# Probabilities and MLP rows transposed in 32x32 blocks by VectorE in a two-layer decode kernel

## The chip, the cores and the metric

The kernel runs on one core of one Trainium2 chip. The metric is the device time of one execution in microseconds (us). Three runs of the kernel before gave a median of 722.28 us (722.20 to 722.33). A difference of 0.2% (1.4 us) is about what such runs can tell from no change.

## The reference

Four tokens (batch B = 4, one position each) of width D = 640 go through attention, MLP, attention, MLP, each behind a layer norm and added to the residual. Both attentions use the same cache and weights, and both MLPs the same weights. All data are fp32.

```python
# Hq = Hkv = 32, Dh = 128, Sk = 4096, W = 1024 (the last 1024 positions of the cache)
def _A_ref(x, k_cache, v_cache, wq, wo):
    q = (x @ wq).reshape(B, 1, 32, 128).transpose(0, 2, 1, 3)
    k, v = k_cache[:, :, Sk - W:, :], v_cache[:, :, Sk - W:, :]
    p = softmax(einsum("bhqd,bhkd->bhqk", q, k) * Dh ** -0.5)
    return einsum("bhqk,bhkd->bhqd", p, v).transpose(0, 2, 1, 3).reshape(B, 1, 4096) @ wo
def _B_ref(x, w1, w2):                      # w1: 640 x 1728, w2: 1728 x 640
    return einsum("bsf,fd->bsd", maximum(einsum("bsd,df->bsf", x, w1), 0), w2)

x = x + _A_ref(layernorm(x), ...); x = x + _B_ref(layernorm(x), ...)
x = x + _A_ref(layernorm(x), ...); x = x + _B_ref(layernorm(x), ...)
```

The keys of each head differ per batch entry, so one head needs four products of one row with 128 x 1024 keys, and four of one row of 1024 probabilities with 1024 x 128 values.

## The kernel before, in words

**Data.** The host packs each head into a record of 128 partitions by 9472 columns (REC): the head's part of wq (columns 0 to 640), the keys (640 to 4736, in two halves), the values (4736 to 8832, in two halves) and the head's part of wo (8832 to 9472). That is 4736 KB. The program reads 32 records for layer 0, then w1 and w2, then 27 records for layer 1 and w1 and w2 again.

**Buffers.** Five slots hold a record each; a `ring` of RING columns holds the weights of the first MLP and some pieces of layer 1. The last five heads of layer 0 stay in their slots, and layer 1 begins with these (the resident heads). The sixth head of layer 1 comes into the ring, in the pieces of IN_RING, while the first MLP still runs; the seventh to the eleventh come in pieces into whatever part of slots and ring has become free. From the twelfth head on whole records go into slots again; the first of them, into slot 2, needs room that the sixth and the seventh head use to their end.

**Order.** Every engine's instructions are chained in the order in which the code is written (class `InOrder`, whose line L81 stands on nearly every row of the profile). All loads are issued by SP, one after another in the fixed list `items`. `pump()` issues the next as soon as its columns are free in the program's order: `done(...)` behind each group of matmuls frees them. A load whose room isn't free holds up all behind it.

**One head.** `query` multiplies the normalized x (columns `xT`) with wq: the result has the four batch rows, split over four column groups of the PE array. VectorE scales it (`qs`), `query_T` transposes it on PE, and a VectorE sum over the groups gives the columns `qT`. `scores` does eight 128x512 matmuls into `sc_ps`, VectorE takes the maximum, ScalarE the exponentials with their sum (`exponentials`, into `prob`). `weights_T` transposes the probabilities with eight PE transposes, `values` multiplies them with the value blocks (`o_ps`), VectorE divides by the sum (`on`), `output_T` transposes with four PE transposes, and `project` adds to `acc`, which stays in PSUM and collects the layer's residual. The loop in `decode_kernel` is software-pipelined: `scores` of the next head is ahead of `values` of this one, and `query` is two heads ahead.

**MLP.** `center` subtracts the mean, `mlp` does x @ w1 into PSUM, relu by ScalarE into SBUF, PE transposes of the hidden rows, and 54 weight tiles of w2 (TILES). `busy` issues matmuls whose result is not used, between the real ones.

Of the kernel before, what the change touches and what calls it, by code (L numbers as in the profile page):

```python
# [47 lines left out]
NS = 5  # L49

TILES = [(f, n) for t in range(4) for f in range(t, 13, 4) for n in range(NB)]
# [3 lines left out]
RING = 4 * FF + 5 * FD  # L55

W1_RING = [0, FF, 2 * FF, 3 * FF, 0]
W2_RING = [(5, 4 * FF), (10, FF), (11, FF + 10 * FD), (11, FF + 21 * FD), (10, 0), (3, FF), (4, FF + 3 * FD)]
# [30 lines left out]
def decode_kernel(ctx: ExitStack, tc: tile.TileContext, xf, rec, w1, w2, out):  # L89
# [5 lines left out]
    ident = sb.tile([P, P], F32, name="ident")  # L95
    mean_of = sb.tile([P, P], F32, name="mean_of")
    xT = sb.tile([P, FD], F32, name="xT")
    prob = sb.tile([P, W], F32, name="prob")
    hidden = prob[:, :512]
    xc = prob[:, 512:512 + FD]  # L100
    square = prob[:, 768:768 + FD]
    pT = sb.tile([P, 2, B, 4], F32, name="pT")
    on = sb.tile([P, 4 * DH], F32, name="on")
    x_sb = on[:, :FD]
    ones = on[:, 2 * P:3 * P]
    hT = on[:, FD:FD + 4 * NB * B].rearrange("p (t j b) -> p t j b", t=4, j=NB)
    oTs = sb.tile([P, LATE, B], F32, name="oTs")
    qs = sb.tile([P, DH], F32, name="qs")
    qT = sb.tile([P, B, 4], F32, name="qT")
    small = sb.tile([P, 24], F32, name="small")  # L110
    nmax, rtot, rstd, eps, unused, sums, squares, tot0, tot1 = (small[:, i:i + 1] for i in range(9))
    var, std, raw = (small[:, i:i + B] for i in (12, 16, 20))
# [4 lines left out]
    sc_ps = ps.tile([P, W], F32, name="sc_ps")  # L117
    pt_ps = [ps.tile([P, 4, P], F32, name=f"pt_ps{i}") for i in range(2)]
    o_ps = ps.tile([P, 512], F32, name="o_ps")
    q_ps = ps.tile([P, 512], F32, name="q_ps")  # L120
# [4 lines left out]
    for n in range(NB):  # L125
        act.dma_start(x_sb[32 * n:32 * n + B], xf[B * n:B * n + B])
    pool.memset(ident, 1.0)
    pool.affine_select(ident, ident, pattern=[[1, P]], compare_op=OP.is_equal, fill=0.0, base=0, channel_multiplier=-1)

    folded = ident.rearrange("p (j s) -> p s j", j=NB).unsqueeze(1).to_broadcast([P, NB, 32, NB])  # L130
    dve.tensor_reduce(mean_of.rearrange("p (j s) -> p j s", j=NB), folded, op=OP.add, axis=AX.X)
    dve.tensor_scalar(mean_of, mean_of, 1.0 / D, None, op0=OP.mult)
    dve.memset(small, EPS)
    dve.memset(q_ps[:, :DH], 0.0)
    dve.memset(sc_ps, 0.0)
    dve.memset(o_ps, 0.0)

# [105 lines left out]
    def busy(n):  # L243

        pe.matmul(sc_ps[0:1, :n], ident[:, 0:1], slot[home(LAST, 0)][:, K:K + n], start=True, stop=True)

    def center(fill):

        x = acc[:, :FD]
        dve.memset(ones, 1.0)  # L250
# [9 lines left out]
        act.activation(square, xc, AF.Square, accum_out=squares)  # L260
        dve.tensor_copy(x_sb, x)

    def scale(before_exp):
# [3 lines left out]
        if before_exp:  # L267
            act.activation(unused, eps, AF.Exp)

    def scale_columns():  # L270

        dve.tensor_scalar(var, mean_of[:, :B], squares, None, op0=OP.mult)
        pe.matmul(o_ps[:, :B], ones, var, start=True, stop=True)
        act.activation(std, o_ps[:, :B], AF.Sqrt, bias=eps, scale=1.0)
# [4 lines left out]
    def residual():  # L279
        pe.matmul(acc[:, :FD], ident, x_sb, start=True, stop=False, skip_group_check=True)  # L280

    def query(r, h, first=False):
        key = ("rec", r, h)
        for k in range(KB):
            j = 32 * (k % NB)
            pe.matmul(q_ps[j:j + B, :DH], xblock(k), cols(key, WQ + k * DH, DH),
                      start=(k < NB), stop=(0 < k % NB or k == NB), skip_group_check=True)
        done(key, WQ, K)
        if first:
            scale_columns()  # L290
            dve.tensor_copy(qs, q_ps[:, :DH])
            dve.reciprocal(std, std)
        else:
            dve.tensor_scalar(qs, q_ps[:, :DH], rstd, DH ** -0.5, op0=OP.mult, op1=OP.mult)

    def query_T(first=False):
        pe.transpose(misc[:, :P], qs, ident)
        q = misc[:, :P].rearrange("p (j s) -> p s j", j=NB)[:, :B, :]
        if first:
            scale(True)  # L300
            dve.tensor_reduce(raw, q, op=OP.add, axis=AX.X)
            raw4, std4 = (a.unsqueeze(2).to_broadcast([P, B, 4]) for a in (raw, std))
            dve.scalar_tensor_tensor(qT, raw4, DH ** -0.5, std4, op0=OP.mult, op1=OP.mult)
            dve.reciprocal(rstd, rstd)
        else:
            dve.tensor_reduce(qT, q.unsqueeze(2).to_broadcast([P, B, 4, NB]), op=OP.add, axis=AX.X)

    def scores(r, h):
# [6 lines left out]
        dve.tensor_reduce(nmax, sc_ps, op=OP.max, axis=AX.X, negate=True)  # L315

    def exponentials(s):
        act.activation(prob, sc_ps, AF.Exp, bias=nmax, scale=1.0, accum_out=tot[s])

    def weights_T(i):  # L320
        for c in range(4):
            pe.transpose(pt_ps[i][:, c, :], prob[:, 512 * i + 128 * c:512 * i + 128 * c + 128], ident)
        dve.tensor_copy(pT[:, i], pt_ps[i].rearrange("p c (b s) -> p b c s", b=B)[:, :, :, 0])

    def values(r, h, s):
        key = ("rec", r, h)
        for i in range(2):
            for b in range(B):
                pe.matmul(o_ps[32 * b:32 * b + 4, :], pT[:, i, b, :], cols(key, V + VH * i + 512 * b, 512),
                          start=(i == 0), stop=(i == 1))  # L330
            done(key, V + VH * i, V + VH * i + VH)
        dve.reciprocal(rtot, tot[s])
        dve.tensor_scalar(on, o_ps, rtot, None, op0=OP.mult)

    def output_T(i):

        for c in range(4):
            pe.transpose(misc[:, P * c:P * c + P], on[:, DH * c:DH * c + DH], ident)
        m = misc[:, :]
        picked = bass.AP(tensor=m.tensor, offset=m.offset, ap=[m.ap[0], [32, B], [P + 1, 4]])  # L340
        dve.tensor_reduce(oTs[:, i], picked, op=OP.add, axis=AX.X)
# [8 lines left out]
    def mlp(r):  # L350
        h_ps = pt_ps[0].rearrange("p c n -> p (c n)")
        for k in range(KB):
            for j in range(NB):
                n = min(512, FF - 512 * j)
                pe.matmul(h_ps[32 * j:32 * j + B, :n], xblock(k), cols(("w1", r), k * FF + 512 * j, n),
                          start=(k == 0), stop=(k == KB - 1))
            done(("w1", r), k * FF, k * FF + FF)
            if k == 0:
                scale(False)
                dve.reciprocal(rstd, rstd)  # L360
                residual()
# [113 lines left out]
```

## Time and profile before

| | |
|---|---|
| median of three runs | 722.28 us (722.20 to 722.33) |
| profiled execution | 722.16 us, its span 720.2 us |
| PE (matmul) busy | 533.4 us, 74% of the span |
| VectorE busy | 208.9 us, 29% |
| ScalarE busy | 90.8 us, 13% |
| DMA queue of SP | 98.9% of 16 engines' span, 303.91 MB |
| HBM read | 303.84 MB, 422 GB/s over the span |
| mean granted PE clock | 0.853 |

The profiled execution's own time is 1.96 us longer than its span, which goes from the first to the last instruction. The names in the rows are those of the kernel's tiles without numbers: `slot<-rec` is a load of a record or a part of one, `ring<-w` one of MLP weights into the ring, `sc_ps` the scores, `pt_ps` the transposed probabilities or the hidden rows, `o_ps` the values' product, `misc` the transposes of `qs` and `on`, `acc` projection or w2. PE is TensorE's matmuls, PEld its weight loads, DVE VectorE, ACT ScalarE.

### The profile page before, as it was taken

Reading aid. Unit: us, or ns where it says so; the run is one execution under the profiler, and the core shown is the slowest. Engines: PE = TensorE matmul, PEld = TensorE weight load, DVE = VectorE, ACT = ScalarE, POOL = GpSimd, SP = SyncE. Lnnn points to the kernel's source line nnn. Section 1 sums busy time; section 2 is a strip of 40 time slices with the busy share of each in tenths; the row PEclk is TensorE's granted clock in tenths of the full one; section 3 lists DMA queues with packets and bytes.
Section 4 is the critical chain, followed back from the end, with each engine's and each line's share of the span. In section 5 each row is a group of like instructions: output and inputs, shape, how many; then the busy total and the mean of one; then the engine's idle time right before and its main releaser. Section 6 shows DMA issues by size and latency. Waiting matters only on the chain.

```text
span 720.2 us, 9962 instructions
## 1 busy us (share of the span) xinstructions
PE 533.4 (74%) x4428; PEld 220.2 (31%) x4428; DVE 208.9 (29%) x554; ACT 90.8 (13%) x156; POOL 0.7 (0%) x6
## 2 busy tenths in 40 slices
PE   3466767668676777767989889785767768677888
PEld 1132323223223232323324333232322323233332
DVE  3222232232332323233422343422223232232430
ACT  2101010110110101011111121201011010110110
POOL 0000000000000000000000000000000000000000
PEclk9778787887886878788999999987788888787999
DMA  9999999999999999999999999999999999999996
GB/s 375 433 437 437 435 433 422 426 432 436 436 433 422 426 436 437 432 430 417 420 401 395 416 429 428 438 432 432 426 431 434 432 432 430 426 432 422 428 420 274
DMA packets 15194, 304.54 MB, mean 423 GB/s; under 512 B 1697, under 2 KB 1969, under 8 KB 5297
## 3 DMA queue, kind: packets, MB, share of 16 engines
q1 hardware_dynamic: 15120, 303.91, 98.9%
q8 instruction: 34, 0.56, 0.3%
q14 instruction: 8, 0.06, 0.0%
q10 hardware_dynamic: 32, 0.01, 0.0%
HBM read 303.84 MB, written 0.08 MB: 422 GB/s over the span
## 4 chain that ended last, share of the span: by engine, by line
DMA 77%; PE 19%; DVE 2%; issue 1%; ACT 0%; SPq 0%; DVEq 0%; ACTq 0%
DMA slot<-rec 76%; PE sc_ps L81 4%; PE acc L81 4%; PE o_ps L81 3%; PE misc L81 3%; PE pt_ps L81 3%; PE q_ps L81 2%; DVE on L81 1%; DMA ring<-w 1%; DVE oTs L81 1%; DVE small L81 0%; ACT prob L81 0%; SPq L81 0%; SPq L78 0%; ACT small L81 0%
## 5 line engine op out<-in xcount | busy, mean ns | idle before, releaser
L81 PE MATMUL q_ps<-slot,xT 128*4 128x128 f32 x620 | 46.9, 317 | 142.4 <-DMA slot<-rec 141.5
L81 ACT ACTIVATE prob<-sc_ps,small 128x1024 f32<-128x1024 f32 x64 | 71.3, 1115 | 563.6 <-DVE small L81 547.8
L81 PE MATMUL sc_ps<-slot,qT 128*4 128x512 f32 x992 | 134.0, 663 | 1.3 <-ACT prob L81 0.7
L81 PE MATMUL o_ps<-slot,pT 128*4 128x512 f32 x1014 | 120.6, 592 | 2.3 <-DMA slot<-rec 1.3
L81 DVE TENSOR_REDUCE small<-sc_ps 128x1 f32<-128x1024 f32 x64 | 78.4, 1224 | 129.7 <-PE sc_ps L81 129.7
L81 PE MATMUL pt_ps<-ident,prob 128*128 128x128 f32 x518 | 112.6, 362 | 0.0
L81 PEld LDWEIGHTS pt_ps<-ident,prob 128*128 128x128 f32 x518 | 83.3, 188 | 29.3 <-issue 28.3
L81 PEld LDWEIGHTS q_ps<-slot,xT 128*4 128x4 f32 x620 | 20.7, 88 | 197.9 <-DMA slot<-rec 185.5
L81 DVE TENSOR_SCALAR qs<-q_ps,small 128x128 f32<-128x128 f32 x62 | 21.6, 348 | 141.4 <-PE q_ps L81 141.4
L81 PE MATMUL misc<-ident,on 128*128 128x128 f32 x256 | 54.6, 350 | 9.5 <-DVE on L81 9.5
L81 DVE COPY pT<-pt_ps 128x16 f32<-128x16 f32 x128 | 22.1, 174 | 122.5 <-PE pt_ps L81 122.5
L81 DVE TENSOR_SCALAR on<-o_ps,small 128x512 f32<-128x512 f32 x64 | 48.0, 750 | 30.2 <-PE o_ps L81 30.2
L81 PEld LDWEIGHTS o_ps<-slot,pT 128*4 128x4 f32 x1014 | 25.3, 87 | 83.7 <-issue 76.5
L81 PE MATMUL acc<-slot,oTs 128*4 128x160 f32 x512 | 38.3, 383 | 16.2 <-DVE oTs L81 16.2
L81 PEld LDWEIGHTS misc<-ident,on 128*128 128x128 f32 x256 | 34.7, 172 | 31.5 <-DVE on L81 16.9
L81 PEld LDWEIGHTS sc_ps<-slot,qT 128*4 128x4 f32 x992 | 20.8, 89 | 70.1 <-issue 64.7
L81 PE MATMUL misc<-ident,qs 128*128 128x128 f32 x64 | 23.6, 368 | 1.1 <-DVE qs L81 1.1
L81 PE MATMUL sc_ps<-slot,ident 128*1 128x512 f32 (+1 forms) x54 | 22.5, 513 | 0.0
L81 DVE TENSOR_REDUCE oTs<-misc 128x4 f32<-128x16 f32 x64 | 11.2, 174 | 33.3 <-PE misc L81 33.3
L81 PEld LDWEIGHTS acc<-slot,oTs 128*4 128x4 f32 x512 | 7.1, 84 | 36.5 <-DVE oTs L81 35.7
L81 DVE TENSOR_REDUCE qT<-misc 128x16 f32<-128x64 f32 x62 | 13.9, 224 | 2.4 <-PE misc L81 1.0
L81 PEld LDWEIGHTS misc<-ident,qs 128*128 128x128 f32 x64 | 12.6, 198 | 2.1 <-DVE qs L81 2.0
(59 smaller groups left out, 108.9 us busy)
## 6 DMA issues: line engine op xcount, KB each, us to landing
slot<-rec SPq DMA_DIRECT2D x46, 4736.0 KB, 31.2
slot<-rec SPq DMA_DIRECT2D x17, 2368.0 KB, 20.7
slot<-rec SPq DMA_DIRECT2D x5, 1024.0 KB, 32.7
ring<-w SPq DMA_DIRECT2D x5, 864.0 KB, 13.5
slot<-rec SPq DMA_DIRECT2D x2, 2048.0 KB, 42.5
slot<-rec SPq DMA_DIRECT2D x3, 1344.0 KB, 7.6
slot<-w SPq DMA_DIRECT2D x3, 864.0 KB, 31.3
ring<-rec SPq DMA_DIRECT2D x1, 2368.0 KB
```

The costliest lines, as they stand in the source:

```text
L81: r = build(*args, **kwargs)
```

## The change

- **Scores.** The query is computed as columns: wq is the stationary operand and x the moving one, so `misc` gets the 128 x 4 result and one VectorE copy makes `qT`. `scores` broadcasts one query column to 32 stationary columns, so that each batch entry fills 32 equal rows. The layer norm's scale and Dh ** -0.5 move into the exponential (`scale=rstd`), with one VectorE product for the bias. There are two buffers `sc_ps`, and the exponentials stay in PSUM.
- **Probabilities.** `weights` replaces `weights_T`: two VectorE transposes of 128x512 in 32x32 blocks from PSUM to PSUM (`t_ps`), each followed by a product with `mrt`, which holds 1 / sum and a mask of the batch entry. A value block then holds 32 keys of each of the four batch entries, and `values` has 16 stationary columns.
- **Output.** `values` leaves four diagonal blocks in `o_ps`; four VectorE instructions pick and add them (`on`), and one matmul with the matrix `pick` replaces four transposes.
- **MLP.** x @ w1 in four equal quarters of 432 columns; relu in PSUM; two VectorE transposes (224 and 256 columns) instead of four PE transposes and two copies; w2 packed to match.
- **Residual.** `acc` simply stays in PSUM; the copy `x_sb` and the matmul `residual` of each layer go.
- **Ring.** 8960 columns instead of 7712, in the room of `prob`, `ident` and others. The five w1 blocks have places of their own, w2 pieces and IN_RING are laid out anew, with six ring pieces (8320 columns) of the sixth head where there were five (7296).

PE in two heads of layer 1 before. `pt_ps` are the probability transposes, `misc<-ident,on` those of the output, `misc<-ident,qs` that of the query:

```order
L81 MATMUL o_ps<-slot_73,pT 4x512 x8
L81 MATMUL q_ps<-slot_75,xT 4x128 x5
L81 MATMUL misc<-ident,on 128x128 x4
L81 MATMUL acc<-slot_73,oTs 4x160 x4
L81 MATMUL pt_ps_78<-ident,prob 128x128 x4
L81 MATMUL misc<-ident,qs 128x128
L81 MATMUL pt_ps_79<-ident,prob 128x128 x4
L81 MATMUL sc_ps<-slot_75,qT 4x512 x8
L81 MATMUL o_ps<-slot_74,pT 4x512 x8
L81 MATMUL q_ps<-slot_71,xT 4x128 x5
```

And the same place now:

```order
L85 MATMUL sc_ps_77<-slot_74,qT 32x512 x8
L85 MATMUL o_ps<-slot_73,scratch 16x512 x8
L85 MATMUL misc<-xT,slot_75 128x4 x5
L85 MATMUL o_ps<-pick,scratch 128x4
L85 MATMUL acc<-slot_73,oTs 4x160 x4
L85 MATMUL sc_ps_78<-slot_75,qT 32x512 x8
L85 MATMUL o_ps<-slot_74,scratch 16x512 x8
```

The thirteen transposes of a head are gone, one `pick` matmul is new, and a head's projection is followed at once by the `scores` of the next but one.

VectorE in one head of layer 1 before, from the maximum of the scores (`small<-sc_ps`) on:

```order
L81 TENSOR_REDUCE small<-sc_ps 128x1
L81 RECIPROCAL small<-small 128x1
L81 TENSOR_SCALAR on<-o_ps,small 128x512
L81 TENSOR_SCALAR qs<-q_ps,small 128x128
L81 TENSOR_REDUCE oTs<-misc 128x4
L81 COPY pT<-pt_ps_78 128x16
L81 TENSOR_REDUCE qT<-misc 128x16
L81 COPY pT<-pt_ps_79 128x16
```

And now, where `scratch` is `on` in the block pick (128x128) and the stationary weights `wT` in the products (128x64):

```order
L85 TENSOR_REDUCE small<-sc_ps_78 128x1
L85 TENSOR_TENSOR small<-small 128x1
L85 TENSOR_SCALAR scratch<-o_ps,of_block 128x128
L85 SCALAR_TENSOR_TENSOR scratch<-o_ps,of_block,scratch 128x128 x3
L85 RECIPROCAL small<-small 128x1
L85 TENSOR_SCALAR mrt<-of_batch,small 128x4
L85 STREAM_TRANSPOSE t_ps<-sc_ps_78 128x512
L85 TENSOR_TENSOR scratch<-t_ps,mrt 128x64
L85 STREAM_TRANSPOSE t_ps<-sc_ps_78 128x512
L85 TENSOR_TENSOR scratch<-t_ps,mrt 128x64
L85 COPY qT<-misc 128x4
L85 COPY oTs<-o_ps 128x4
```

Eight instructions became fourteen, and `oTs` (this head's output, which `project` reads) now stands last, behind the next head's transposes.

The diff, cut to its core:

```diff
-TILES = [(f, n) for t in range(4) for f in range(t, 13, 4) for n in range(NB)]
+TILES = [(m, n) for m in range(13) for n in range(NB)]
-RING = 4 * FF + 5 * FD
+RING = 5 * FF + 2 * FD
-W1_RING = [0, FF, 2 * FF, 3 * FF, 0]
+W1_RING = [0, FF, 2 * FF, 3 * FF, 4 * FF]
-IN_RING = [(0, 1664, FF + 10 * FD), (1664, 3200, FF + 21 * FD), (3200, 4224, FF + 21 * FD + 1536),
-           (4224, 5760, 0), (5760, 7296, 1536)]
+IN_RING = [(0, 1152, 7680), (1152, 3200, 640), (3200, 4736, 2688), (4736, 6272, 4224), (6272, 7808, 5760),
+           (7808, 8320, 0)]
...
+    def query(r, h):
+        key = ("rec", r, h)
         for k in range(KB):
+            pe.matmul(misc[:, 8:8 + B], cols(key, WQ + k * DH, DH), xblock(k), start=(k == 0), stop=(k == KB - 1))
         done(key, WQ, K)
+        dve.tensor_copy(qT, misc[:, 8:8 + B])
...
-                pe.matmul(sc_ps[32 * b:32 * b + 4, 512 * i:512 * i + 512], qT[:, b, :],
+                pe.matmul(sc_ps[s][32 * b:32 * b + 32, 512 * i:512 * i + 512], qT[:, b:b + 1].to_broadcast([P, 32]),
...
+        dve.tensor_tensor(nmax, nmax, rstd, op=OP.mult)
+        act.activation(sc_ps[s], sc_ps[s], AF.Exp, bias=nmax, scale=rstd, accum_out=tot[s])
+
+    def weights(s):
+        dve.reciprocal(rtot, tot[s])
+        dve.tensor_scalar(mrt, of_batch, rtot, None, op0=OP.mult)
+        for i in range(2):
+            dve.transpose(t_ps, sc_ps[s][:, 512 * i:512 * i + 512])
+            dve.tensor_tensor(wT[:, i], t_ps.rearrange("p (c j) -> p c j", j=32)[:, :, :B],
+                              mrt.unsqueeze(1).to_broadcast([P, 16, B]), op=OP.mult)
...
-        dve.reciprocal(rtot, tot[s])
-        dve.tensor_scalar(on, o_ps, rtot, None, op0=OP.mult)
+        dve.tensor_scalar(on, o_ps[:, :DH], of_block[:, 0:1], None, op0=OP.mult)
+        for c in range(1, 4):
+            dve.scalar_tensor_tensor(on, o_ps[:, DH * c:DH * c + DH], of_block[:, c:c + 1], on, op0=OP.mult, op1=OP.add)
     def output_T(i):
+        pe.matmul(o_ps[:, :B], on, pick, start=True, stop=True)
+        dve.tensor_copy(oTs[:, i], o_ps[:, :B])
...
         for n, h in enumerate(hs):
             more = n + 1 < H
             i = n - (H - late)
             if more:
+                scores(r, hs[n + 1], (n + 1) % 2)
+            values(r, h)
+            if more:
+                weights((n + 1) % 2)
             if n + 2 < H:
                 query(r, hs[n + 2])
             if i < 0:
                 output_T(0)
                 project(r, h, 0, False)
```

More of the change, by code (lines that the diff above doesn't have):

```diff
@@ L243, in busy @@
     def busy(n):
-        pe.matmul(sc_ps[0:1, :n], ident[:, 0:1], slot[home(LAST, 0)][:, K:K + n], start=True, stop=True)
+        pe.matmul(sc_ps[1][0:1, :n], mean_of[:, 0:1], slot[home(LAST, 0)][:, K:K + n], start=True, stop=True)
     def center(fill):
         x = acc[:, :FD]
-        dve.memset(ones, 1.0)
         dve.tensor_reduce(sums, x, op=OP.add, axis=AX.X)
@@ L276, in xblock, with scale_scores @@
+    def scale_scores():
+        pe.matmul(o_ps[:, 8:8 + B], ones.to_broadcast([P, P]), mrt, start=True, stop=True)
+        dve.tensor_tensor(mrt, o_ps[:, 8:8 + B], of_batch, op=OP.mult)
+        dve.tensor_reduce(sums, mrt, op=OP.add, axis=AX.X)
+        act.activation(rstd, sums, AF.Sqrt, bias=eps_dh, scale=float(DH))
+        act.activation(unused, eps, AF.Exp)
     def xblock(k):
         return xT[:, 32 * k:32 * k + B]
[L279 to L280 removed]
@@ L320, in weights_T @@
[L320 to L325, printed above, removed]
+        dve.tensor_reduce(nmax, sc_ps[s], op=OP.max, axis=AX.X, negate=True)
+        if first:
+            dve.reciprocal(rstd, rstd)
+        dve.tensor_tensor(nmax, nmax, rstd, op=OP.mult)
+        act.activation(sc_ps[s], sc_ps[s], AF.Exp, bias=nmax, scale=rstd, accum_out=tot[s])
@@ L396, in decode_kernel @@
     pump()
-    residual()
+    pe.matmul(acc[:, :FD], ident, x_sb, start=True, stop=False, skip_group_check=True)
     for r in range(2):
@@ L401, in decode_kernel @@
         center(r > 0)
-        query(r, hs[0], True)
-        query_T(True)
-        scores(r, hs[0])
-        exponentials(0)
-        residual()
+        dve.tensor_scalar(mrt, mean_of[:, :B], squares, None, op0=OP.mult)
+        query(r, hs[0])
+        scale_scores()
+        scores(r, hs[0], 0, True)
         query(r, hs[1])
+        weights(0)
         for n, h in enumerate(hs):
```

152 lines of the change are left out of this document (52 added, 100 removed).

## The prediction

> **What bounds the kernel now.** I read the page's slices first, then the chain of waits, then the DMA queue's own issues.
>
> ```profile
> DMA  9999999999999999999999999999999999999996
> GB/s 375 433 437 437 435 433 422 426 432 436 436 433 422 426 436 437 432 430 417 420 401 395 416 429 428 438 432 432 426 431 434 432 432 430 426 432 422 428 420 274
> ...
> slot<-rec SPq DMA_DIRECT2D x46, 4736.0 KB, 31.2
> ```
>
> The DMA engines never rest before the last slice. A record (4736 KB, 4.85 MB) takes 11.3 us at the usual 430 GB/s. It lands 31.2 us after its issue, so it waits some 20 us behind others in the queue. Through most of the program compute could be many microseconds slower and no transfer would start later. The only low slices are numbers 21 and 22 (401 and 395 GB/s), from 360 to 396 us: the MLP of layer 0 and the start of layer 1. There the chain of waits leaves the DMA for compute:
>
> ```profile
> 406.00 1.83 PE sc_ps L81 x16
> ...
> 411.33 0.46 PE acc L81 x8
> ...
> 412.92 1.83 PE sc_ps L81 x16
> ...
> 446.02 0.46 PE acc L81 x8
> ...
> 453.47 26.66 DMA slot<-rec
> ```
>
> These are the resident heads. Layer 1 begins with five heads whose records still lie in the slots, so compute runs ahead at its own pace: 6.92 us a head (412.92 less 406.00), against 11.3 us that the DMA needs for one. The DMA now waits for room, and room comes from finished heads. How much slack is there? The columns are start, length (for several issues, first to last), what.
>
> ```profile
> 425.72 0.33 SPq L81 DMA_DIRECT2D slot<-rec  x1
> ...
> 437.28 0.33 SPq L81 DMA_DIRECT2D ring<-rec  x1
> 437.66 9.21 SPq L81 DMA_DIRECT2D slot<-rec  x2
> ```
>
> The DMA view gives, for the issue at 425.72 and for the program's very first one, KB and us to landing:
>
> ```profile
> slot<-rec SPq DMA_DIRECT2D x1, 2368.0 KB, 20.7
> ...
> slot<-rec SPq DMA_DIRECT2D x1, 2368.0 KB, 8.3
> ```
>
> So the piece issued at 425.72 landed at 446.4. Two more such pieces (437.28 and 437.66) end the queue at 446.4 + 11.3 = 457.7. The next load, the first whole record of layer 1 into slot 2, was issued at 446.5 (second of the two at 437.66), right after the seventh head's output projection (446.02 + 0.46). So it had 457.7 - 446.5 = 11.2 us to spare. The very first DMA takes 8.3 us where 2368 KB in the stream take 5.65, so a restart from an empty queue costs 2.6 us. True slack: 8.6 us. The forecast turns on whether the new heads use it up.
>
> **The larger ring: a gain.** The dips, per 2 us (last number GB/s, the one before DMA share):
>
> ```profile
> 370.00:372.00 2.00, 2.00 (x14) 0.70 (x14) 0.16 (x1) 0.26 (x1) 0.00 (x0) 1.00 0.92 315
> ...
> 382.00:384.00 2.00, 2.00 (x26) 0.72 (x19) 0.00 (x0) 0.00 (x0) 0.00 (x0) 1.00 1.01 411
> 384.00:386.00 2.00, 2.00 (x36) 0.82 (x35) 0.00 (x0) 0.00 (x0) 0.00 (x0) 1.00 1.00 319
> ...
> 388.00:390.00 2.00, 1.96 (x15) 0.75 (x14) 0.55 (x2) 0.00 (x0) 0.00 (x0) 1.00 0.93 357
> ...
> 396.00:398.00 2.00, 1.04 (x9) 0.36 (x13) 0.42 (x2) 1.21 (x2) 0.00 (x0) 1.00 1.00 382
> ```
>
> Against 411 GB/s the four lose 0.47 + 0.45 + 0.26 + 0.14 = 1.3 us. With 8960 columns the fifth w1 block no longer waits for the first, and the first two ring pieces of layer 1 need w2 pieces consumed earlier. I take all 1.3 us as gained (ends 0 and 1.3): the queue's end moves from 457.7 to 456.4.
>
> **The head: a loss.** Rows that price it (mean ns follows the busy time):
>
> ```profile
> L81 DVE TENSOR_REDUCE small<-sc_ps 128x1 f32<-128x1024 f32 x64 | 78.4, 1224 | 129.7 <-PE sc_ps L81 129.7
> L81 DVE TENSOR_SCALAR on<-o_ps,small 128x512 f32<-128x512 f32 x64 | 48.0, 750 | 30.2 <-PE o_ps L81 30.2
> L81 DVE COPY pT<-pt_ps 128x16 f32<-128x16 f32 x128 | 22.1, 174 | 122.5 <-PE pt_ps L81 122.5
> L81 DVE TENSOR_SCALAR qs<-q_ps,small 128x128 f32<-128x128 f32 x62 | 21.6, 348 | 141.4 <-PE q_ps L81 141.4
> L81 DVE TENSOR_REDUCE qT<-misc 128x16 f32<-128x64 f32 x62 | 13.9, 224 | 2.4 <-PE misc L81 1.0
> L81 DVE RECIPROCAL small<-small 128x1 f32<-128x1 f32 x68 | 10.4, 153 | 4.5 <-ACT small L81 4.5
> L81 DVE STREAM_TRANSPOSE xT<-prob 128x160 f32<-128x160 f32 x4 | 1.4, 345 | 0.1
> L81 DVE TENSOR_SCALAR small<-mean_of,small 128x4 f32<-128x4 f32 x2 | 0.4, 214 | 0.0
> L81 ACT ACTIVATE prob<-sc_ps,small 128x1024 f32<-128x1024 f32 x64 | 71.3, 1115 | 563.6 <-DVE small L81 547.8
> L81 PEld LDWEIGHTS misc<-small,mean_of 128*128 128x128 f32 x8 | 1.4, 219 | 2.4 <-DVE small L81 2.4
> ```
>
> Two rows of the timeline give the delays behind `scores` (it began at 406.00) and `values`:
>
> ```profile
> 407.96 1.22 DVE L81 TENSOR_REDUCE small<-sc_ps 128x1 f32<-128x1024 f32 x1 [1.76 <-PE sc_ps L81]
> 409.61 0.75 DVE L81 TENSOR_SCALAR on<-o_ps,small 128x512 f32<-128x512 f32 x1 [0.35 <-PE o_ps L81]
> ```
>
> Removed on PE: eight probability transposes, one of q, four of the output. But the new order is serial on VectorE: the output copy `oTs`, for which the projection and everything behind it on PE wait, stands behind the next head's `weights`. Count from the start of `scores`. VectorE begins the maximum at 1.96 (407.96 - 406.00) and ends at 3.18; the product with `rstd`, 0.15 and 0.03 of gap: 3.36. `values` is done at 3.61 (409.61 - 406.00). The block pick is one 128x128 TENSOR_SCALAR (0.35) and three two-input ones at 0.35 + 0.03: 5.10. The exponential (1.12, accumulator about 0.2) ends at 4.7 and hides there; writing PSUM it might be 0.3 slower and still hide. Reciprocal and mask 0.15 + 0.21 + 0.06: 5.52. Two 128x512 transposes: 0.345 for 160 columns plus 352 at 1.05 ns (750 less 348 over 384 columns) gives 0.71; in proportion it would be 1.10, at two columns a cycle 0.53. I take 0.71, as the column price is that of rows next to it. Each is followed by a 64-element product, 0.22 + 0.06: together 1.98, so 7.50. Two small copies 0.34, a semaphore 0.05, projection 0.4 (0.46 in the chain, but the next starts before its end): the next `scores` begins at **8.3 us**. The query by columns needs ten 128x128 weight loads, 0.22 us for one alone; in a row I take 0.15, so 1.5 us (upper end 2.2). It ends at 5.0 and the pick matmul at 5.5. Both hide under VectorE, and in the steady state under the 20 us queue.
>
> **The clock.** That leaves PE idle from 5.5 to 7.8 in every resident head, 2.3 us. Full-clock windows of the trace, which come every 3.41 us (columns: PE busy, PEld, DVE, ACT, POOL, granted clock):
>
> ```profile
> 93.14:96.56 3.42, 1.73 (x23) 0.97 (x24) 0.88 (x3) 0.42 (x2) 0.00 (x0) 1.00 1.00 432
> 96.56:99.97 3.41, 3.41 (x17) 1.78 (x20) 0.57 (x3) 0.00 (x0) 0.00 (x0) 0.50 1.06 456
> ...
> 478.85:482.27 3.42, 1.83 (x24) 1.07 (x25) 0.83 (x3) 0.38 (x2) 0.00 (x0) 1.00 0.98 421
> 482.27:485.68 3.41, 3.41 (x33) 1.35 (x35) 1.00 (x4) 0.00 (x0) 0.00 (x0) 1.00 0.98 422
> ...
> 439.09:446.02 6.93, 6.21 (x63) 1.00 1.01 429
> ```
>
> and from the timeline the longest gap (in brackets) in the first of these windows:
>
> ```profile
> 94.56 0.60 PE L81 MATMUL q_ps<-slot,xT 128*4 128x128 f32 x10 [1.91 <-DMA slot<-rec]
> ```
>
> With 1.73 us busy the next window had half the clock; with 1.83 it kept it. So over 1.68 us of idle time in a window costs the next one. An idle block of 2.3 us puts that much into one window for 2.35 of 3.41 positions, 69%: four heads of six. The throttled window falls on the next `scores` and `values` (3.66 us of work) and does 1.7 of its 3.41 us: **1.7 us late**. Before, PE was busy 6.21 us of a resident head's 6.93 (the row of 439.09, PE alone) and kept the clock.
>
> [...]
>
> **The sum.** The third head's `scores` now starts at 406.00. I take 405.3: w2 ends 1.2 earlier, PE's filler matmuls give 0.3 of it back, and the first two heads' longer chain 0.2 (ends 404.7 and 406.5). Six heads: 405.3 + 6 x 8.3 = 455.1; four throttled, + 6.8: 461.9; restart 2.6: 464.5, where before that record began at 457.7. **+6.8 us.** Later records are released every 9 to 10 us, under 11.3, so nothing more is lost.
>
> At nothing: one more ring piece for SP to issue (0.33 us, as in its rows above, with a queue behind it), the MLP by VectorE transposes, the residual in PSUM. The end is DMA-timed, by the chain and then the timeline:
>
> ```profile
> 714.11 2.54 PE acc L81 x60
> ```
> ```profile
> 716.69 0.11 PEld L81 LDWEIGHTS acc<-slot,on 128*4 128x4 f32 x8 [0.38 <-DMA slot<-w]
> ```
>
> The last eight w2 matmuls wait for their weights, and the filler ahead of 714.11 absorbs about 1.7 us; without that cover the last head's longer block pick would show as 0.7. The profiled execution took 722.16 us for a span of 720.2; 722.16 + 6.8 = 729.0, and the median is 0.12 higher: **729.1 us**.
>
> **Rivals.** *No throttling:* the record begins at 455.1 + 2.6 = 457.7, as before: 722.3, and up to 724 with slower VectorE rows. For it: PE's weight loads for the query may count as activity. Against: the idle block alone passes 1.68 us. *Faster:* the head costs 8.1 us or less and keeps its clock; the release then comes before 456.4 and the ring's 1.3 us stays: 720.9. It decides at (456.4 - 2.6 - 405.3) / 6 = 8.08 us; my 8.3 is close, which is for it. *Compute takes over:* transposes at 1.10 (+0.8) and two throttled windows a head (+3.4) give 12.5 us, above 11.3: 25 us lost on six heads and 1.2 us on each of the 24 after, about 775. Against it: a full window at half clock restored it (96.56 above).
>
> **Numbers.** Forecast 0.66, no throttling 0.18 (0.14 of it within 0.2%, 1.4 us, which is about what a measurement tells from no change; 0.04 slower), faster 0.10, compute takes over 0.06. Faster 0.10, same 0.14, slower 0.76. The range goes from the ring's gain almost whole (721.0) to all six heads throttled (+3.4) and half of the transposes' upper price (6 x 0.39): 734.8. It leaves out the last rival, and most of the faster one.
>
> **What the new profile would show.** Heads between 400 and 465 us at 8.2 to 10 us where they took 6.9; granted clock below 1.00 there; the first whole record into slot 2 issued near 461 with GB/s falling for some microseconds just before its data; no dip at 370 or 385. If the clock stays 1.00 and heads take 8.1, the forecast is wrong by the throttle's 6.8 us; if 512-column transposes take far from 0.71 us, by twelve times the difference.

## The result: 4% slower, and the profile after

| | before | after |
|---|---|---|
| median | 722.25 us (722.20 to 722.33) | 753.58 us (753.13 to 756.64) |
| ratio | | 1.044, 95% interval 1.042 to 1.047 |
| profiled execution, its span | 722.16, 720.2 us | 753.13, 751.4 us |
| mean granted PE clock | 0.853 | 0.768 |
| VectorE busy | 208.9 us | 338.9 us |

The forecast of 729.1 us (721.0 to 734.8) was wrong: 31.2 us came on top of the span, not 6.8. The slices of the page after, with the same columns as before:

```profile
DMA  9999999999999999999939997999999999999991
GB/s 388 426 441 420 442 428 420 446 423 428 437 424 437 431 422 443 424 424 423 387 125 407 366 432 319 414 428 422 440 427 432 432 424 437 431 426 424 423 420 64
```

There are now three holes: slices 20 and 21 (387 and 125 GB/s, the end of layer 0), slices 23 to 25 (366 and 319, the resident heads), and the last slice (64). How much is each worth? Two stretches before, then two after that begin at the same times; the second is longer after, since its work ends later. The columns are the stretch, its length, busy time of PE, PEld, VectorE, ScalarE and GpSimd, then granted clock, DMA share, GB/s:

```profile
360.00:402.00 42.00, 37.87 (x342) 13.94 (x342) 9.84 (x33) 8.54 (x19) 0.00 (x0) 1.00 1.01 398
402.00:470.00 68.00, 57.49 (x586) 24.20 (x579) 27.62 (x73) 10.85 (x18) 0.00 (x0) 0.99 1.01 430
```
```profile
360.00:402.00 42.00, 34.25 (x261) 11.26 (x262) 12.21 (x37) 4.42 (x10) 0.00 (x0) 0.76 0.70 271
402.00:492.00 90.00, 68.57 (x519) 29.05 (x517) 48.86 (x138) 15.16 (x25) 0.00 (x0) 0.87 0.94 387
...
737.00:740.00 3.00, 3.00 (x21) 0.68 (x20) 0.00 (x0) 0.00 (x0) 0.00 (x0) 1.00 0.01 3
```

End of layer 0: 42 us at 271 instead of 398 GB/s is 42 x 127 / 430 = 12.4 us of transfers not made. Resident heads: 90 us at 387 where the stream made 430, 90 x 43 / 430 = 9.0 us. The tail: from 737 us on hardly anything lands (3 GB/s), but the output leaves at 748.9 us:

```profile
748.88 0.35 SPq L85 DMA_DIRECT2D out<-scratch  x1
```

Before, it left at 717.57 us, right behind the last w2 matmuls, which had waited for their weights. The tail is the rest: 31.2 - 12.4 - 9.0 = 9.8 us. These sizes are those of one execution. In a run below whose layer 0 is the changed kernel's own (oTs first, the rest of layer 1), the stretch of 360 to 402 us had 319 GB/s, a hole of 7.7 us.

What do the three places share? The chain of waits after, from the last heads of layer 0 to its first w1 matmuls (start, length, what; the trace has two records for each fp32 matmul of the code, so x16 are the eight of `scores`):

```profile
345.16 3.04 PE sc_ps L85 x16
348.20 2.13 PE o_ps L85 x16
352.21 0.64 DVE t_ps L85
353.13 0.74 DVE t_ps L85
354.32 0.46 PE acc L85 x8
354.77 2.42 PE sc_ps L85 x16
...
363.94 3.64 PE sc_ps L85 x16
...
374.17 3.66 PE o_ps L85 x16
...
380.00 1.18 PE acc L85 x16
...
382.53 4.03 PE sc_ps L85 x12
```

The DMA is no part of this stretch. One head goes from `scores` (345.16) over `values`, VectorE's two transposes (`t_ps`) and the projection (`acc`) to the next `scores` (354.77): 9.6 us. The last w1 and w2 pieces wait for what these heads and the first w1 matmuls free. The second w2 piece was issued at 386.6 us, where it was issued at 371.7 before:

```profile
386.64 0.33 SPq L85 DMA_DIRECT2D ring<-w  x1
```
```profile
371.69 0.33 SPq L81 DMA_DIRECT2D ring<-w  x1
```

The resident heads, by the `scores` rows of the same chain:

```profile
420.24 3.02 PE sc_ps L85 x16
...
429.85 1.72 PE sc_ps L85 x16
...
437.82 3.35 PE sc_ps L85 x16
...
447.36 2.84 PE sc_ps L85 x16
...
457.23 3.41 PE sc_ps L85 x16
...
467.37 1.72 PE sc_ps L85 x16
...
475.31 3.38 PE sc_ps L85 x16
```

Steps of 9.6, 8.0, 9.5, 9.9, 10.1 and 7.9 us: about 8.0 where `scores` ran at full clock (1.72), 9.5 to 10.1 where it didn't. And where TensorE stands still inside a head (timeline, idle time in brackets):

```profile
427.14 0.25 PE L85 MATMUL o_ps<-pick,scratch 128*128 128x4 f32 x1
429.39 0.46 PE L85 MATMUL acc<-slot,oTs 128*4 128x160 f32 x8 [2.00 <-DVE oTs L85]
```

Two microseconds between the `pick` matmul and the projection, waiting for `oTs`, which VectorE copies only after the next head's `weights`. The VectorE rows that answer to those the forecast was priced from (mean ns after the busy time):

```profile
L85 DVE STREAM_TRANSPOSE t_ps<-sc_ps 128x512 f32<-128x512 f32 x128 | 93.2, 728 | 2.2
...
L85 DVE SCALAR_TENSOR_TENSOR scratch<-o_ps,of_block,scratch 128x128 f32<-128x128 f32 x192 | 67.3, 351 | 6.8
L85 DVE TENSOR_SCALAR scratch<-o_ps,of_block 128x128 f32<-128x128 f32 x64 | 22.4, 350 | 50.6 <-PE o_ps L85 50.6
...
L85 DVE TENSOR_TENSOR scratch<-t_ps,mrt 128x64 f32<-128x64 f32 x128 | 28.8, 225 | 4.4
```

### The profile page after: what moved, and what is told of

It is laid out like the page before. It is cut to its first block, busy times and chain, and to the rows that moved or that the text cites. A ratio compares the mean times of both kernels' runs of the same rounds, so it can differ in the third digit from the quotient of the medians.

```text
span 751.4 us, 8825 instructions
## 1 busy us (share of the span) xinstructions
PE 538.2 (72%) x3704; PEld 222.6 (30%) x3704; DVE 338.9 (45%) x934; ACT 96.0 (13%) x154; POOL 1.1 (0%) x9
## 4 chain that ended last, share of the span: by engine, by line
DMA 55%; PE 29%; DVE 13%; issue 1%; ACT 0%; another core or an unknown queue 0%
DMA slot<-rec 55%; PE sc_ps L85 13%; PE o_ps L85 8%; DVE scratch L85 6%; DVE t_ps L85 4%; PE acc L85 4%; PE misc L85 4%; DVE mrt L85 1%; DVE small L85 1%; DVE oTs L85 1%; ACT sc_ps L85 0%; DVE qT L85 0%; DVE sc_ps L85 0%
## 5 line engine op out<-in xcount | busy, mean ns | idle before, releaser
L85 PE MATMUL sc_ps<-slot,qT 128*32 128x512 f32 x992 | 200.6, 951 | 2.9 <-DVE oTs L85 2.0
L85 PE MATMUL misc<-xT,slot 128*128 128x4 f32 x620 | 98.7, 286 | 123.4 <-DMA slot<-rec 122.5
L85 ACT ACTIVATE sc_ps<-sc_ps,small 128x1024 f32<-128x1024 f32 (+3 forms) x70 | 77.5, 1107 | 593.1 <-DVE small L85 571.0
L85 PE MATMUL o_ps<-slot,scratch 128*16 128x512 f32 x1010 | 149.8, 715 | 2.7 <-DVE oTs L85 1.9
L85 PEld LDWEIGHTS misc<-xT,slot 128*128 128x128 f32 x620 | 93.3, 233 | 178.5 <-DMA slot<-rec 160.0
L85 DVE STREAM_TRANSPOSE t_ps<-sc_ps 128x512 f32<-128x512 f32 x128 | 93.2, 728 | 2.2
L85 PEld LDWEIGHTS o_ps<-slot,scratch 128*16 128x16 f32 x1010 | 37.4, 126 | 137.8 <-issue 131.8
L85 DVE SCALAR_TENSOR_TENSOR scratch<-o_ps,of_block,scratch 128x128 f32<-128x128 f32 x192 | 67.3, 351 | 6.8
L85 PEld LDWEIGHTS sc_ps<-slot,qT 128*32 128x32 f32 x992 | 43.6, 155 | 80.1 <-issue 71.9
L85 PE MATMUL o_ps<-pick,scratch 128*128 128x4 f32 x128 | 29.1, 298 | 15.5 <-DVE scratch L85 15.5
L85 DVE COPY qT<-misc 128x4 f32<-128x4 f32 x64 | 10.1, 157 | 50.8 <-PE misc L85 50.5
L85 PE MATMUL sc_ps<-slot,mean_of 128*1 128x512 f32 (+1 forms) x54 | 26.2, 590 | 0.0
L85 DVE RECIPROCAL small<-small 128x1 f32<-128x1 f32 x68 | 10.4, 153 | 8.8 <-ACT small L85 7.5
L85 DVE COPY oTs<-o_ps 128x4 f32<-128x4 f32 x64 | 10.1, 158 | 7.7 <-PE o_ps L85 6.7
```

The source lines that it names most:

```text
L85: r = build(*args, **kwargs)
```

## Experiments

Theory A: heads that are not paced by the DMA are paced by VectorE's serial chain, with the half clock on top, and this happens at all three places. Rivals: B, the layer ends are slow through the new MLP chain and the new ring; C, VectorE's new work is too slow in any order; D, the half clock is the whole loss. All ratios are against runs of the kernel before on the same chip (medians of 722.3 to 722.9 us).

| kernel | median us | ratio (95%) |
|---|---|---|
| after | 753.58 | 1.0443 (1.0415 to 1.0470) |
| oTs first, all heads | 727.36 | 1.0055 (1.0037 to 1.0073) |
| oTs first, layer 0 | 745.63 | 1.0321 (1.0270 to 1.0371) |
| oTs first, 12 heads of layer 1 | 742.35 | 1.0268 (1.0236 to 1.0301) |
| oTs first, the rest of layer 1 | 746.53 | 1.0342 (1.0299 to 1.0385) |
| after + long fillers | 1138.47 | 1.573 (1.568 to 1.578) |
| after + short fillers | 733.25 | 1.0131 (1.0079 to 1.0182) |
| after + third transpose | 766.25 | 1.0601 (1.0577 to 1.0625) |
| after + 32-column query | 749.18 | 1.0362 (1.0342 to 1.0383) |
| oTs first + old ring | 729.80 | 1.0084 (1.0056 to 1.0112) |
| oTs first + 32-column query | 725.62 | 1.0042 (1.0028 to 1.0056) |
| oTs first + fillers at the ends | 722.83 | 1.0009 (0.9995 to 1.0023) |
| the same, and after the 27th head | 722.61 | 0.9996 (0.9987 to 1.0005) |
| the same + 32-column query | 722.42 | 0.9998 (0.9988 to 1.0007) |
| before, residual stays in acc | 722.31 | 0.9996 (0.9988 to 1.0005) |

### The order on VectorE, everywhere and by place

```diff
             values(r, h)
-            if more:
-                weights((n + 1) % 2)
             if n + 2 < H:
                 query(r, hs[n + 2])
             if i < 0:
                 output_T(0)
-                project(r, h, 0, False)
             elif more:
                 output_T(i)
+            if more:
+                weights((n + 1) % 2)
+            if i < 0:
+                project(r, h, 0, False)
```

TensorE's order does not change; on VectorE the copies `qT` and `oTs` now stand ahead of the two transposes.

> Only VectorE's order changes: the output copy oTs and the next query copy stand ahead of the next head's two transposes instead of behind them. Theory A (serial order on VectorE): a head then costs VectorE's own sum, 1.24 + 0.15 + 4 x 0.35 + 2 x 0.16 + 0.36 + 2 x 0.73 + 2 x 0.23 = about 5.5 us plus waits, so 6.0 to 6.5 us a head instead of 8 to 10; TensorE is then busy over 80% and keeps its clock, and all three losses go (11.6 us at the end of layer 0, 9.4 in the resident heads, 10.0 at the end): 721 to 724 us. Theory B (the layer-end losses come from the new MLP chain and the new ring, not from the heads): only the 9.4 us go, 743 us. Theory C (the transposes and products are too slow in any order): heads stay near 8 us and the time above 740.

Measured: 727.36 us, 26.2 of the 31.3 us gone. One resident head in its chain of waits:

```profile
424.49 1.72 PE sc_ps L85 x16
426.21 1.76 PE o_ps L85 x16
427.99 0.36 DVE scratch L85
...
429.56 0.40 PE o_ps L85 x2
430.20 0.46 PE acc L85 x8
430.65 1.72 PE sc_ps L85 x16
```

This head takes 6.16 us (430.65 less 424.49), less than the 6.92 us of the kernel before, with the same instructions as in the changed kernel. Of its neighbours in the chain, those whose `scores` ran at full clock took 6.2 to 6.4 us and two at half clock 7.5 and 7.8. The transposes have left the chain. B and C fall as the main cause. The forecast of the time was 3.4 us too low, and the clock was not kept everywhere as it said (mean 0.786, 0.853 before); what remained is below.

The same edit for one place each (`r == 1 and n < 12`, `r == 0`, `r == 1 and n >= 12`):

> The reordering of the first kernel of this set, only in the first twelve heads of layer 1. Theory A: the 9.4 us of the resident heads go and the rest stays: 743.7 us; the queue still runs empty before the fifth w2 piece of layer 0 and the end is still 10.9 us behind the last landing. If the three losses hang together (a late start of layer 1 costs again later), less or more than 9.4.

> The reordering only in layer 0. Theory A: its last heads are no longer late, the second ring piece of w2 is issued near 372 instead of 386.6, and 11.6 us go: 741.5 us, with the resident heads' 9.4 and the tail's 10.0 unchanged. Theory B (the new MLP chain and ring make that hole): about 753.

> The changed kernel with the reordering only from the 13th head of layer 1 on. Theory A: the last heads are no longer late, the output leaves 1 to 3 us behind the last landing instead of 10.9, the losses of layer 0 and of the resident heads stay: 743 to 746 us. If the tail's loss were made by the MLP chain: 753.

Measured 742.35, 745.63 and 746.53 us: 11.2, 8.0 and 7.1 us less than the changed kernel. Together 26.3, as much as the edit gives everywhere (26.2). Each of the three gains is clear of zero, so at all three places the order of the heads costs time. By the intervals each gain is uncertain by 3 to 4 us and their sum by some 8, so that they add up is shown only so far, and the match to 0.1 us is luck. The first was forecast well (743.7 us), the second was not: 741.5 us were expected, and layer 0 gave back 8.0 of 12.4 us, since the reordered heads still end late there. The third is just above its 743 to 746 us.

### The clock alone

Matmuls whose result is not used, in TensorE's 2.0 us gap, in the changed kernel's own order. First ten of 384 columns into `misc`:

```diff
                 output_T(0)
+                keep_clock()
                 project(r, h, 0, False)
```

> The changed kernel in its own order, with ten matmuls of 384 columns whose result is not used (about 1.7 us) in each head between the pick matmul and the projection, where TensorE idles 2.0 us. Theory A: the clock stays 1.00, heads cost 8.0 us each instead of 8.0 to 10.5; some 8 us go at the end of layer 0, 7 in the resident heads, 7 at the end: about 730 us, and the serial order still costs 7 to 9. Rival D (the half clock is the whole loss): 722 to 724. Rival E (the fillers only delay the projection, or do not hold the clock): 753 or more.

A miss of the experiment: 1138 us. Here is one head's gap in its timeline:

```profile
443.32 9.06 PE L85 MATMUL misc<-mean_of 128*1 128x384 f32 x19 [1.93 <-DVE qT L85]
```

The fillers took 9.1 us, not 1.7, and began only when the gap was over: the row has VectorE's `qT` copy, which reads `misc`, as what released them after 1.93 us of idle time. I had priced them from `scores`, whose 16 records of 512 columns take 1.72 us, 0.11 us each: in the changed kernel's trace they start in fours, four within 20 ns (467.188 to 467.208 us) and the next four 0.43 us after these. A filler took 0.48 us (9.06 / 19). The second try, at the same place, puts seven of 160 columns (moving `xT`) into free columns of `acc`, which no VectorE instruction in a head reads. With them the kernel's output changed, by a relative error of 0.54; all other instructions and all transfers are as in the changed kernel.

> The changed kernel in its own order, with seven matmuls of 160 columns (about 1.6 us at full clock, result not used, into columns of acc that nothing reads) in each head between the pick matmul and the projection, where TensorE idles 2.0 us. Theory A (serial order and clock both cost): heads 8.0 us each at full clock, about 730 us. Rival D (the half clock is the whole loss): 722 to 724. Rival E (fillers of this kind do not hold the clock): 753.

Measured 733.25 us at a mean clock of 0.860. Its resident heads:

```profile
412.24 1.72 PE sc_ps L85 x16
...
420.15 1.72 PE sc_ps L85 x16
...
428.06 1.72 PE sc_ps L85 x16
```

7.91 us a head, at full clock in these and in most of the others; one further on, from 443.88 us, lost the clock, and it and the next took 17.4 us together. So holding the clock gave back 20 of the 31 us, and 11 us are left, either of them uncertain by some 4 us. The fillers take as long as the gap (2.0 us), and longer where the clock is lost (3.44 us in the chain of the head from 443.88 us, with a part of its projection), so 11 us is rather an upper end for the serial order alone. D falls, since it asked for 722 to 724 us; A stands, with both parts. The reordering takes most of TensorE's 2.0 us gap away along with the serial time.

### More work on VectorE

```diff
     dve.transpose(t_ps, sc_ps[s][:, 512 * i:512 * i + 512])
+    if i:
+        dve.transpose(t_ps, sc_ps[s][:, 512 * i:512 * i + 512])
```

> The changed kernel with a third 128x512 transpose in each head (the second one done twice), 0.73 us of VectorE more. Theory A (VectorE's serial chain sets the pace wherever the queue does not): every compute-paced head is 0.73 us longer: 4 at the end of layer 0, some 7 resident ones, 4 at the end, 15 x 0.73 = 11 us: 764 us. Rival G (only the clock of TensorE sets the pace and VectorE's time is hidden): 753 to 755.

Measured 766.25 us, 12.7 more than the changed kernel, near the 11 us expected at 0.73 us for each of 15 heads. The total agrees better than its parts do. In the chain of this run the heads from 422.8 to 476.3 us took 10.4 to 11.5 us where the changed kernel's resident heads took 7.9 to 10.1, and none of them had its `scores` at full clock (3.1 to 3.4 us). So part of the 12.7 us is clock, and this run does not price VectorE's time alone; the short fillers above, with the clock held, are the better sign that it is not hidden.

### What halves the clock

The mark from the kernel before (at most 1.73 us busy in a window) does not hold in the new heads. Four windows of the changed kernel, two and two, and what filled the first window that lost the clock:

```profile
427.33:430.74 3.41, 1.41 (x21) 0.63 (x24) 1.90 (x6) 0.00 (x0) 0.00 (x0) 1.00 0.87 371
430.74:434.15 3.41, 3.41 (x33) 1.41 (x25) 2.12 (x5) 0.98 (x1) 0.00 (x0) 1.00 0.98 344
451.22:454.63 3.41, 2.87 (x24) 1.61 (x16) 2.34 (x9) 1.30 (x2) 0.00 (x0) 1.00 1.04 439
454.63:458.04 3.41, 1.52 (x16) 0.69 (x20) 1.73 (x6) 0.00 (x0) 0.00 (x0) 0.50 1.05 441
```
```profile
450.82 1.68 PE L85 MATMUL o_ps<-slot,scratch 128*16 128x512 f32 x12
452.42 1.28 PE L85 MATMUL misc<-xT,slot 128*128 128x4 f32 x10
454.12 0.39 PE L85 MATMUL o_ps<-pick,scratch 128*128 128x4 f32 x2 [0.42 <-DVE scratch L85]
```

1.41 us of busy PE kept the clock, 2.87 us lost it. In the second window 1.28 us were the query's ten matmuls, which move only 4 columns each behind a 128x128 weight load (1.19 us of PEld in these 1.28), and the `pick` is of the same kind; without them 1.27 us are left. In the changed kernel's trace the 60 windows that lost a full clock held at most 1.36 us of matmuls of more than 4 columns, and the 53 that kept it at least 1.35. In other runs the two sides lie elsewhere: at 1.73 and 1.82 us in the kernel before, and less sharply apart with the third transpose, where a window with 1.53 us lost the clock, and with short fillers, where one with 1.33 us kept it. The test moves more columns and nothing else (the five matmuls of a query are ten in the trace):

```diff
-            pe.matmul(misc[:, 8:8 + B], cols(key, WQ + k * DH, DH), xblock(k), start=(k == 0), stop=(k == KB - 1))
+            pe.matmul(misc[:, 8:40], cols(key, WQ + k * DH, DH), xT[:, 32 * k:32 * k + 32], start=(k == 0), stop=(k == KB - 1))
```

> The changed kernel in its own order, with one edit: the ten query matmuls of a head move 32 columns instead of 4 (the other 28 belong to empty rows and are not read). Each still hides under its weight load of 0.13 us, so a query takes the same 1.28 us of TensorE and the idle gaps stay. In all windows of 3.41 us seen so far the next window was halved when matmuls other than those of 4 columns had been busy for at most 1.3 to 1.4 us, even where TensorE as a whole was busy for 2.9. Theory H (the clock gate does not count the 4-column matmuls, which are nearly all weight load): with 32 columns each query counts about 0.4 us more, many windows pass the mark, fewer heads run at half clock: 735 to 748 us at a mean clock above 0.80. Rival I (the gate goes by idle time, or by any busy time): nothing changes, 753 us at 0.77.

> The reordered kernel (oTs ahead of the transposes) with 32-column query matmuls. Theory H: its single heads at half clock among the resident heads and at the end of layer 0 get rarer, mean clock above 0.82 where it was 0.786, 723 to 726 us. Rival I: 727.4 at 0.786.

Measured: 749.18 us, mean clock 0.790 to 0.799 in its four executions where it was 0.768 to 0.776, with order and gaps as they were; and 725.62 us in the reordered kernel against 727.36. The first is 4.4 us faster than the changed kernel (intervals apart), but just outside theory H's 735 to 748 us and not above its 0.80. The better evidence is a window of the first run and the one behind it:

```profile
467.51:470.92 3.41, 2.77 (x24) 1.61 (x16) 2.22 (x9) 1.29 (x2) 0.00 (x0) 1.00 1.01 433
470.92:474.34 3.42, 1.66 (x24) 0.73 (x28) 1.60 (x6) 0.00 (x0) 0.00 (x0) 1.00 0.66 215
```

It holds the same work as the window at 451.22 above: `o_ps`, a query, a `pick`. TensorE is busy for less of it (2.77 us for 2.87), the gap ahead of `pick` is the same (0.40 us for 0.42), and yet it kept the clock. So between these two windows neither idle time nor busy time decided; what differs is the columns that the query's ten matmuls move, 32 for 4 each. The effect is smaller than expected: this window held 1.14 us of matmuls wider than the query, where the changed kernel's mark was 1.35, so by an estimate from these two numbers a query counts for some 0.2 us, not 0.4. The second run is not clear of no effect: its interval overlaps that of the reordered kernel, and its clock (0.776 to 0.808, median 0.799, against 0.774 to 0.797, median 0.785) stayed below the 0.82 that theory H forecast.

### The ring, the last heads, the residual

```diff
-RING = 5 * FF + 2 * FD
+RING = 4 * FF + 5 * FD
-W1_RING = [0, FF, 2 * FF, 3 * FF, 4 * FF]
+W1_RING = [0, FF, 2 * FF, 3 * FF, 0]
```

W2_RING and IN_RING are those of the kernel before, too.

> The first reordered kernel (oTs ahead of the transposes) with the ring's constants of the kernel before: 7712 columns, fifth w1 block behind the first, five pieces of the sixth head. In the reordered kernel the queue runs empty for some 4 us at the end of layer 0, since the second w2 piece waits for the first w1 block. Theory R (the larger ring gains): the fifth w1 block now waits for that too, the hole opens one w1 block and 320 - 0 columns of w2 earlier, 2.1 + 0.4 us: about 730 against 727.4. My forecast had 1.3 us for it: 728.7. Rival: the ring is hidden, 727.4.

729.80 against 727.36 us has the expected sign and size, but the two intervals overlap (1.0056 to 1.0112, 1.0037 to 1.0073): not settled.

In the reordered kernel, slices of time at the end of layer 0 show what was left:

```profile
366.00:372.00 6.00, 4.55 (x26) 1.14 (x26) 2.62 (x8) 0.00 (x0) 0.00 (x0) 0.50 1.02 416
372.00:378.00 6.00, 6.00 (x33) 1.81 (x33) 1.22 (x4) 1.71 (x3) 0.00 (x0) 0.50 0.51 206
378.00:384.00 6.00, 6.00 (x41) 1.50 (x40) 0.16 (x1) 0.26 (x1) 0.00 (x0) 0.95 0.67 235
```

A hole of (430 - 206 + 430 - 235) x 6 / 430 = 5.8 us, with half clock from 366 to 378 us. The faster heads waited 2.5 us for the last record's first half (wq and keys) and came out of that wait throttled: the next `scores` took 3.64 us, where those at full clock took 1.90. `fill(n)` issues n matmuls of 160 columns into `misc`; three to six more stand in each later gap:

```diff
             values(r, h)
+            if n == H - 3:
+                fill(4 if r else 10)
+            if n == H - 2:
+                fill(5)
...
```

> The first reordered kernel, with matmuls of 160 columns whose result is not used in the gaps of TensorE in the last three heads of each layer (10 ahead of the last query, where TensorE waited 2.5 us for a DMA in layer 0, and 3 to 6 in the gaps of 0.8 to 1.8 us behind it). Theory A with the clock: the last scores of layer 0 and the last values take 1.9 us instead of 3.6 and the first w1 matmuls keep the full clock, so the hole of some 4 us in the queue closes and the end is no longer 2 us late: 721.5 to 723. Rival F (the serial chain of the last head alone makes the hole): 726 to 728. Rival E (the fillers delay more than they hold): above 728.

Measured 722.83 us: 4.5 us won, level with before.

The next version has the first condition as `n == H - 3 or (r == 0 and n == H - 6)`:

> As the reordered kernel with fillers at the layers' ends, with ten fillers also ahead of the query that is two heads ahead of the 27th head of layer 0, where TensorE waited 3.9 us for a DMA and came out of it at half clock. In that kernel the heads from 332 to 350 us ran at a granted clock of 0.69, so the fillers ahead of the last query ended 2.8 us after its data was there, and the second w2 piece was issued at 375.25 with 2.6 us of queue left: a hole of about 2 us. Theory A: now the last query starts when its data lands (354.5), that piece is issued near 371, the hole closes, and the larger ring's gain shows: 720.3 to 721.3, 0.2% faster than before. Rival: the hole has another cause (the ring's order), 722.5 to 723.

Measured 722.61 us. The expected 0.2% did not come: ten fillers behind the 27th head did not hold the clock (0.50 in 343.8 to 347.2 us, behind a window with 2.72 us busy of which 1.28 were a query).

The same with 32-column queries:

> The reordered kernel with fillers at the layers' ends and ahead of the query after the 27th head of layer 0, now with 32-column query matmuls. In the version with 4 columns the clock stayed half from 333 to 347 us, behind a window with 2.33 us of TensorE time of which nearly 1 us was a query, and the second w2 piece was issued at 374.5. Theory H: full clock from 327 on, that piece issued near 371, no hole in the queue: 720.3 to 721.5 us, 0.2% faster than before. Rival I: 722.6, as with 4 columns.

Measured 722.42 us. The piece was issued at 372.8 and the hole is nearly closed:

```profile
366.00:372.00 6.00, 5.67 (x58) 2.50 (x58) 2.62 (x8) 0.94 (x3) 0.00 (x0) 1.00 1.02 420
372.00:378.00 6.00, 6.00 (x44) 1.57 (x40) 0.17 (x1) 1.04 (x2) 0.00 (x0) 1.00 0.98 367
378.00:384.00 6.00, 5.36 (x60) 1.94 (x56) 0.83 (x3) 1.08 (x3) 0.00 (x0) 1.00 1.01 413
```

The time is still that of the kernel before (0.9998, 0.9988 to 1.0007), as rival I had it, and not the 720.3 to 721.5 us of theory H. The DMA makes up 71% of this kernel's chain of waits and 77% of the kernel before's, and the ring's 1.3 us are not to be seen in the time. No version here beats the kernel before.

The residual alone, in the kernel before:

```diff
-        dve.tensor_copy(x_sb, x)
...
-                residual()
```

> The kernel before, with the one part of the change that stands alone: the residual simply stays in acc, without the copy to x_sb and the identity matmul of each layer part. My forecast put it at nothing, since other work hides it: 722.3 to 722.6, within 0.1% of before. Rival: it shortens the chain from the last heads to w1 in the dip around 370 us, by up to 0.5 us: 721.9.

Measured 722.31 us, ratio 0.9996: nothing, as forecast.

## Why the prediction was wrong, point by point

**What bounds the kernel** (DMA, with the resident heads as the exception): half right. The resident heads lost 9.0 us, forecast 6.8. But they are not the only place where compute sets the DMA.

**The failed step is "At nothing ... the end is DMA-timed", with 0.7 us without cover, and its twin, which the sum leaves out: the last heads of layer 0.** I took the last heads of both layers as paced by the DMA. In front of each MLP there are heads in a row that the new order makes 8 to 11 us long, and behind them the w1 matmuls start late. That was worth 12.4 and 9.8 us in the profiled execution, some 70% of the whole, and the reordering in layer 0 alone and in the later heads of layer 1 alone gave back 8.0 and 7.1 us. The 0.7 us counted one pick of one head. The half clock, which I priced for the resident heads alone, was part of it: holding it everywhere gave back 20 of the 31 us. The profile of before had the sign: I read the dips at 370 and 384 us as a matter of the ring, but a dip there says that the DMA already waited for compute at the end of layer 0, so there was little slack left for longer heads.

**The larger ring, 1.3 us gained:** not seen. In the changed kernel the holes cover it; with the holes closed the time is before's. One comparison points to 2.4 us, within its uncertainty.

**The head, 8.3 us:** right, 7.9 to 8.0 measured at full clock. The prices held (728 ns for 710, 351 for 350, 225 for 220, query 1.28 us for 1.5; the exponential in PSUM took 1177 ns in the mean and 1115 into `prob` before, 0.06 us more where 0.3 was allowed for), and the serial order was named as the reason; the reordering shows it.

**The clock, 1.7 us in four of six heads:** four of six heads were throttled, and by 1.5 to 2.1 us. The reason was off, so the right count is luck: the mark of 1.73 us of busy PE is one of the old heads. The window at 451.22 had 0.54 us of idle time in all, its longest gap 0.42 us, and was still followed by one at half clock; 1.28 of its 2.87 us of busy PE were a new query's matmuls.

**The sum of the resident heads, 6.8 us:** 9.0 measured. The heads and their throttling took 55.1 us for six, where the sum had 56.6. What was mis-sized is the start: the third head began at 420.2 us, not 405.3, and 12.4 of these 14.9 us are layer 0's hole, which moves the queue back as well. The other 2.5 us less the 1.5 us of the heads make 1.0 of the 2.2 us between 6.8 and 9.0; the rest was not taken apart.

**Rivals:** "no throttling" and "faster" did not occur; the weight loads, which might have spoken for the first, did not hold the clock with 1.61 us of PEld in the window at 451.22. "Compute takes over" (775 us) did not occur either: it asked for heads of 12.5 us, above the 11.3 us of a record, and the heads stayed below that. It was still the only rival in which compute costs time outside of the resident heads; the place that counted, the ends of the layers, stood in none, and the range had no room for it.

## What to carry to other kernels

A head that is well hidden in the steady state is not hidden at the ends of a layer, where the last loads are cut so that compute can follow quickly: look for every dip in GB/s in the profile before the change, and price a longer head at each of them. When work moves to an engine that runs its instructions in the order of the code, as all do in this kernel (`InOrder`), check what the other engine waits for behind it: here two small copies moved ahead of two transposes were worth 26 of 31 us without an instruction less. Then look at the clock once more, since faster heads can wait longer for the DMA and come out of the wait at half clock, as here at the end of layer 0 (2.5 us of wait, then `scores` in 3.64 us).

## What the runs showed of the hardware

- In the changed kernel's trace 60 windows of 3.41 us at full clock were followed by one at half clock and 53 by another at full clock. How long PE was busy did not separate them: 2.87 us with a 4-column query lost the clock, and 1.41 us, nearly all of 160- and 512-column matmuls, kept it. The busy time of matmuls of more than 4 columns nearly did: at most 1.36 us where the clock was lost, at least 1.35 where it was kept. With a 32-column query (the changed kernel with that one edit) a window with 2.77 us busy kept it. The marks are those of this run: in the kernel before the two sides lie at 1.73 and 1.82 us, and single windows of 1.53 us lost the clock (third transpose) and of 1.33 us kept it (short fillers).
- Faster heads lost the clock where slower ones kept it: the reordered kernel waited 2.5 us for a record at 352 us, and its next `scores` took 3.64 us, where those of the kernel before, whose heads are slower, took 1.90.
- With the short fillers (matmuls with the start flag set, into columns of `acc` that nothing reads) the kernel's output changed, by a relative error of 0.54. No run here shows why.
